# Batch 0's plain attention in two steps: q of two visits turned together, its last tokens' values behind a fifth w_in piece

## Chip, core and metric

The kernel runs on one core of one Trainium2 chip. The metric is the device time of that core, in microseconds (us), as the median of three runs. A core has TensorE (matmuls), VectorE, ScalarE and GpSimd (elementwise work) and a queue of DMA transfers that SyncE issues. In the profile they are called PE (its weight loads PEld), DVE, ACT, POOL and SP. Each engine works through its own list of instructions in order, and waits for the others by semaphores.

## What is computed

Attention over 8 batches, 8 heads, 576 tokens and 64 columns per head, and then a feed-forward layer over the 4608 tokens:

```python
scores = scale * np.matmul(q, k.transpose(0, 1, 3, 2))
mask_plain = (rel >= 0) & (rel < window)                     # window 32, heads 0 to 3
mask_dil = (rel >= 0) & (rel < window * dilation) & (rel % dilation == 0)   # dilation 4, heads 4 to 7
...
attn = np.exp(scores)
attn = attn / (np.sum(attn, axis=-1, keepdims=True) + 1e-09)
attn_out = np.matmul(attn, v)
...
h = x @ w_in                      # x: 4608 x 512, w_in: 512 x 2048
out = np.maximum(0.01 * h, h) @ w_out   # w_out: 2048 x 512
```

rel is the distance from a query back to a key, so each query sees 32 keys: the last 32 tokens in the plain heads, every fourth of the last 128 in the dilated ones. The inputs and the output are float32; the kernel multiplies in float16.

## The kernel before

**Stages and tiles.** Two batches make one block of 1152 tokens in `xt`, and a block is cut into three chunks of 384 tokens: chunk 0 holds the first 384 tokens of batch 0, chunk 1 those of batch 1, chunk 2 the last 192 of both. For each chunk, `up` (L778) makes 16 groups of up matmuls, one for each j: each group adds four matmuls of 128x384, one for each of four blocks of 128 rows of w_in (L792), into one of two banks `hps`, and ScalarE's leaky ReLU writes `gt` (L803). `down` (L827) makes three row blocks of 128 tokens, each of 16 matmuls of 128x512 in four parts of four (L841), into one of two banks `fps`; VectorE copies the sum to `osb` (L851), which goes to memory.

Attention of one batch is four visits of two heads, first the dilated pairs (2 and 3), then the plain ones (0 and 1). A visit has three units, u = 0, 1, 2. A unit makes a score bank of 384 columns on TensorE (L685, L669), its exponential on ScalarE (L691), a masking on VectorE (L705) or, for some units, a bias added on TensorE beforehand (L666), the value matmuls (L729, L739, L749) with row sums from a matrix of ones (L717), Ln and Exp on ScalarE for one over the sum (L761, L763), and the product on VectorE, which writes `xt` (L767).

**Batches 0 and 1 are early.** Their load is split: part 0 holds the units u = 0 and 1, which are the first 384 tokens, part 1 the unit u = 2. In part 0 of these two batches the value matmuls are half-width units: two sets of 64 columns side by side (L729 with `64x96` outputs, then L717). The q and k of a visit are cast to float16 in `nat`, turned by TensorE with an identity matrix into a bank (`tp` for q, `tpk` for k of batch 0, L557), and moved from there by VectorE or ScalarE into `slots` (L509, helper `move` at L503), where scores read them. For a plain visit q moves in four copies: two of 64x480 and two of 64x4x8, one of each for each head. The last 64 tokens (512 to 575) of all eight heads come separately: `load_rest` (L389) loads them into `rest`, TensorE turns all at once, and small copies put them into the slots (L583 on). The plain values of one batch are 24 tiles of 128 overlapping rows by 64 columns, six for each head: `load_group` (L306) loads them in two transfers of 12 tiles, one for each visit, as rows of 256 B, and GpSimd casts 12 tiles to `vp` (L379).

**Weights.** w_in comes in eight pieces of 512 KB, w_out in eight. Pieces 0 to 3 of w_in hold the columns of j = 0 to 7, pieces 4 to 7 those of j = 8 to 15, each piece one of the four row blocks. So a group j needs four pieces. Each piece is cast in two halves (L437).

**What sets the order.** All work is entered as tasks in a planner (L61 to L134), which gives each task an estimated duration, a priority and its dependencies, runs the engines' lists through an event loop, and so fixes one order on each engine; the instructions are then emitted in that order. The priority of the attention of a visit is `first + step * n`, with the pairs for batch 0 part 0, batch 0 part 1, batch 1 part 0 and batch 1 part 1 from `RANKS` (L21). The priority of loads of batches 0 and 1 and of all weights is the place in the string `FIRST` (L20, read at L873): b and v are q with k, and v, of one group of batch 0 (dilated first), c and y those of batch 1, i is a w_in piece, o a w_out piece, 0 and 1 the last tokens of batch 0 and batch 1. The masks that VectorE needs come with priority `CON` (L18) behind w_in's seventh piece. Where the planner sees a hole on TensorE before the down matmuls begin, matmuls on a constant tile fill it (L934); nothing reads their result.

**Names that the steps below touch.** `lv` and `v_late` (the loads of v, and what is left for later), `c_v` (the casts of v), `q_to` and `k_to` (the copies out of the turned banks), `turn` (L523) with its part 0 at L614, `unit` (L638). Only one bank, `sps`, holds scores after part 0 of batch 0, and two, `ops`, hold the values.

Of the kernel before, what the change touches and what calls it, by code (L numbers as in the profile page):

```python
# [16 lines left out]
WHEN = (-5.0, 15.0, 50.0, 77.0, 112.0, 138.0, 172.0, 200.0)  # L17
CON = -1484.5  # L18
AFTER = -1495.0
FIRST = "bvbviiii0iicooiicoyoooooy1"  # L20
RANKS = ((10.0, 1.0), (10.0, 3.0), (20.0, 2.0), (40.0, 0.5))  # L21


def _constants():
# [113 lines left out]
def kernel(  # L138
# [44 lines left out]
    def dram(t, off, *dims):  # L183
        return bass.AP(tensor=t.tensor, offset=t.offset + off, ap=[list(d) for d in dims])
# [48 lines left out]
                return n * (ta + (tb - ta) * (size - a) / (b - a)) / 16e3  # L233
        return n * size / 25.6 / 16e3

    def load(queue, dst, src, n, size, deps, prio):
        eng = ENG[queue]
        return plan.dma(queue, 0.7 if size == 128 else 0.48, took(n, size), deps,
                        lambda e: eng.dma_start(dst, src), prio,  # L239
                        LATE if prio > -1500 + len(FIRST) else 0.8 if prio >= AFTER else 0.0)  # L240

# [64 lines left out]
    def load_group(b, g, prio, prio_v):  # L306


        dil = g == 1
        early = b < EARLY  # L310
        first = b == 0
        base = (b * H + 4 * g) * HS
        stage, loads = [], []
        for o, src in ((0, q), (1, k)):
            sn, s_old = ring("STG", NST, s_users := [])
            st = stg[sn]
            if first:
                lo = [load("SP", at(st, 0, 128, j * 512, [256, 2], [1, 256]),
                           dram(src, base + 2 * j * HS, [4 * D, 128], [HS, 2], [1, 256]),
                           256, 1024, s_old, prio + 0.3 * j + 0.1 * o) for j in range(2)]  # L320
            elif early:
                lo = [load("SP", at(st, 0, 128, 0, [256, 4], [1, 256]),
                           dram(src, base, [4 * D, 128], [HS, 4], [1, 256]),
                           512, 1024, s_old, prio)]
            else:
                lo = [load("SP", at(st, 32 * a, 32 * a + 32, 0, [32, 36], [1, 32]),
                           dram(src, base + (a // 2) * 2 * HS + (a % 2) * 32,
                                [D, 32], [32 * D, 36], [1, 32]),
                           1152, 128, s_old, prio) for a in range(4)]
            stage.append((st, s_users))  # L330
            loads.append(lo)

        vn, v_old = ring("VST", NVS, v_users := [])
        vs = vst[vn]
        if dil and early:
            lv = [load("SP", at(vs, 0, 128, 0, [256, 4], [1, 256]),
                       dram(v, base, [4 * D, 128], [HS, 4], [1, 256]), 512, 1024, v_old, prio_v)]
            v_late[b] = vs, v_old, v_users
        elif dil:
            lv = [load("SP", at(vs, 0, 128, i * 256, [512, 4], [1, 256]),  # L340
                       dram(v, base + i * 64 * D, [4 * D, 128], [HS, 4], [1, 256]),
                       512, 1024, v_old, prio_v) for i in range(2)]
        elif early:
            lv = []
            for j in range(2):
                n = 12 - (first and j == 0)
                lj = [load("SP", at(vs, 0, 128, (12 * j + 12 - n) * D, [D, n], [1, D]),
                           dram(v, base + (1152 * j + 96 * (12 - n) - 32) * D, [D, 128], [96 * D, n],
                                [1, D]), 128 * n, 256, v_old, prio_v + 0.3 * j)]
                if n < 12:  # L350
                    lj += [load("SP", at(vs, PAD, 128, 0, [1, D]), dram(v, 0, [D, 96], [1, D]),
                                96, 256, v_old, prio_v), t_vz]
                lv.append(lj)
        else:
            lv = [load("SP", at(vs, 0, 128, 0, [D, 24], [1, D]),
                       dram(v, base - 32 * D, [D, 128], [96 * D, 24], [1, D]),
                       3072, 256, v_old, prio_v)]

        for j in range(2):
            nn, n_old = ring("NAT", NNAT, n_users := [])  # L360
            na, c_qk = nat[nn], []
            for o in range(2):
                st, s_users = stage[o]
                if early:
                    dst = at(na, 0, 128, o * 512, [D, 2], [128, 4], [1, D])
                    src = at(st, 0, 128, j * 512, [256, 2], [D, 4], [1, D])
                    n = 512
                else:
                    dst, src, n = na[:, o * S:o * S + S], st[:, j * S:j * S + S], S
                c_qk.append(cast(dst, src, n, (loads[o][j:j + 1] if first else loads[o]) + n_old, prio,  # L370
                                 (("ACT",) if o else ("DVE",)) if first and dil and j == 0 else
                                 CENG if early else ("POOL",)))
                s_users.append(c_qk[-1])
            dn, d_old = ring("VD" if dil else "VP", NV, d_users := [])
            vt = (vd if dil else vp)[dn]
            n_v = 384 if not dil else 256 if early else 512
            h_a, h_s = (2 * j * n_v, n_v) if early else (j * n_v, 2 * n_v)
            n, w = n_v // D, 128 * (8 if dil else 6)
            c_v = [cast(at(vt, 0, 128, 0, [w, 2], [128, n], [1, D]),  # L379
                        at(vs, 0, 128, h_a, [h_s, 2], [D, n], [1, D]), 2 * n_v,  # L380
                        (lv[j] if early and not dil else lv) + d_old, prio_v)]
            v_users += c_v
            seen_ones[b, 2 * g + j] = [t_ones["d" if dil else "p", dn]]
            kept[b, 2 * g + j] = vt, d_users
            visits[b, 2 * g + j, 0] = (na, c_qk, n_users, vt,
                                       c_v + ([t_one] if (b, 0) in TILED else
                                              [t_ones["d" if dil else "p", dn]]), d_users)

    def load_rest(b, prio):  # L389
# [5 lines left out]
        for o, src in ((0, q), (1, k)):  # L395
# [3 lines left out]
        c = cast(at(rest, 0, 128, 0, [128, 8], [D, 2], [1, D]),  # L399
                 at(st, 0, 128, 0, [D, 8], [0, 2], [1, D]), 1024, lo + r_old, prio)  # L400
        s_users.append(c)
        vs, v_old, v_users = v_late[b]
        spread = bass.AP(tensor=vs.tensor, offset=vs.offset + 1024,
                         ap=[[4 * vs.ap[0][0], 16], [256, 4], [1, 256]])
        lv = load("SP", spread,
                  dram(v, (b * H + 4) * HS + 512 * D, [4 * D, 16], [HS, 4], [1, 256]),
                  64, 1024, v_old + [t_vr], prio)
        for vi in (2, 3, 0, 1):
            vt, d_users = kept[b, vi]
            c_v = []  # L410
            if vi >= 2:
                c_v = [cast(at(vt, 0, 64, 0, [1024, 2], [128, 4], [1, D]),
                            at(vs, 0, 64, 1024 + (vi - 2) * 512, [256, 2], [D, 4], [1, D]), 512,
                            [lv] + d_users, prio + 30)]
                v_users += c_v
            visits[b, vi, 1] = rest, [c], r_users, vt, c_v + seen_ones[b, vi], d_users
# [3 lines left out]
    def load_w(n, prio):  # L420
# [10 lines left out]
        else:  # L431
            x = 1024 * (n - 8)
            src = dram(moe_w_out, 128 * x, [2 * DM, 128], [1, 1024])
            dst = w_out
        t = load("SP", st, src, 128, 4096, old, prio)
        for i in range(2):
            c = cast(dst[:, x + 512 * i:x + 512 * i + 512], st[:, 512 * i:512 * i + 512], 512, [t],  # L437
                     prio, ("POOL",) if 4 <= n < 8 else CENG)
# [71 lines left out]
        cost = {"DVE": 0.1 + n * 0.00065, "ACT": 0.08 + n * 0.00095}  # L510
        return add(tuple((e, cost[e]) for e in eng), None, 0.2, deps, fn, prio)

    slot_of, turned_rest, pair_moves = {}, {}, {}
    held = {t.name: [] for t in banks["S0"] + banks["O0"]}

    def arranged(dil, u0, u1):
# [6 lines left out]
    def turn(b, hp, part, prio):  # L523
# [50 lines left out]
        def k_to(bank, i, p0, p1, lo, hi, deps, eng=("DVE",)):  # L574
            n = hi - lo
            if dil:
                o, od, id_ = lo, [[144, 4], [1, n]], [[128, 4], [1, n]]
            else:
                o, od, id_ = PAD + 4 * lo, [[4, n], [1, 4]], [[1, n], [128, 4]]
            return [move(at(kb, p0, p1, o, *od), at(bank, p0, p1, i, *id_), 4 * n,  # L580
                         deps + old + zk, prio, eng)]

        if part == 1:  # L583
            if hp == 2:
# [26 lines left out]
            q_users += new  # L611
            ev += new
        else:
            _, q_old = ring("TP", 1, q_users := [])  # L614
            tq = add("PE", 0.23, 0.25, c_qk[:1] + [t_id] + q_old, turn_in(tpb, na, 0), prio, 0.2)
            n_users.append(tq)
            for lo, hi in ((0, 128),) if dil else ((0, 120), (120, 128)):
                q_users += q_to((lo, lo), lo, hi, [tq])
            if b == 0:
                _, k_old = ring("TPK", 1, k_users := [])  # L620
                kb_in, c_in, k_eng = tpk, 0, ("DVE", "ACT")
            else:
                k_old, k_users, kb_in, c_in, k_eng = q_old, [], tpb[:, 512:1024], 512, ("DVE",)
            tk = add("PE", 0.23, 0.25, [c_qk[1], t_id] + k_old, turn_in(kb_in, na, 512), prio, 0.2)
            n_users.append(tk)
            k_users += k_to(tpk if b == 0 else tpb, c_in, 0, 128, 0, 128,
# [3 lines left out]
            else:  # L630
                for t in q_users:
                    t.deps.append(tk)
                q_users += k_users
            ev += q_users + k_users
        slot_of[b, hp] = tn, users, ev
        return ev, users, qb, kb

# [347 lines left out]
```

The softmax here doesn't subtract the row's maximum and nothing guards it: scores larger than these inputs give would overflow.

## Time and profile before

The time is 317.56 us, the median of 317.21, 317.56 and 317.59. The profiled run has a span of 314.2 us, with TensorE's full clock granted throughout.

| engine | busy us | share of the span |
|---|---|---|
| TensorE, matmul | 303.7 | 97% |
| TensorE, weight load | 179.6 | 57% |
| ScalarE | 219.7 | 70% |
| VectorE | 174.2 | 55% |
| GpSimd | 120.4 | 38% |

| lines | what | count | busy us |
|---|---|---|---|
| L792 | up matmuls | 824 | 149.9 |
| L841 | down matmuls | 592 | 145.7 |
| L803 | leaky ReLU | 206 | 94.0 |
| L767 | product into xt | 138 | 52.4 |
| L509 | copies into the slots | 47 | 14.4 |

Transfers move 51.14 MB in all. Over the first 60 us they move 18.68 MB, at 311 GB/s on average. A row of a timeline has the start in us from the beginning of the span, the busy time, the engine, the line, the operation, what is written and read, the shape and how many instructions were merged; in brackets, the idle time of the engine just before and what ended it. TensorE's busy time includes the filler of L934 and of L863, so it is no measure of useful work in the first stage.

### The profile page before, as it was taken

How to read it: one execution, taken by the hardware profiler on the slowest of the kernel's cores; microseconds unless marked ns; L12 is line 12 of the kernel's file. 1: busy time of each engine (PE TensorE's matmuls, PEld its weight loads, DVE VectorE, ACT ScalarE, POOL GpSimd, SP SyncE). 2: the span in 40 equal slices, each digit the busy share in tenths (PEclk: the TensorE clock that was granted, in tenths of full speed). 3: DMA queues.
4: the chain of work that ended last, by engine and by line, in shares of the span. 5: the costliest groups of instructions: out<-in, count | busy, mean ns of one | idle time of the engine just before them, and what ended most of it. 6: DMA issues, size and time to landing. Idle time of an engine off the chain costs nothing.

```text
span 314.2 us, 6332 instructions
## 1 busy us (share of the span) xinstructions
PE 303.7 (97%) x2257; PEld 179.6 (57%) x2257; DVE 174.2 (55%) x396; ACT 219.7 (70%) x501; POOL 120.4 (38%) x174
## 2 busy tenths in 40 slices
PE   7968999999999999999999999999999999999995
PEld 3625555667777656655555555555555555555544
DVE  5856894557896687857858667654433420000011
ACT  3925674889998999987888888787887743334310
POOL 4466655464584463935819447450000000000000
PEclk9999999999999999999999999999999999999999
DMA  7999999999999399999989978711111111211113
GB/s 247 326 331 407 401 318 190 259 193 207 239 217 189 119 222 180 229 174 206 192 185 197 179 208 147 169 35 33 35 33 35 33 35 46 53 37 35 33 33 100
DMA packets 158175, 51.14 MB, mean 163 GB/s; under 512 B 139200, under 2 KB 151616, under 8 KB 158144
## 3 DMA queue, kind: packets, MB, share of 16 engines
q1 hardware_dynamic: 157696, 50.46, 67.3%
q8 instruction: 17, 0.28, 0.4%
q10 hardware_dynamic: 448, 0.29, 0.3%
q14 instruction: 14, 0.11, 0.1%
HBM read 41.30 MB, written 9.44 MB: 161 GB/s over the span
## 4 chain that ended last, share of the span: by engine, by line
PE 83%; DMA 7%; ACT 4%; SPq 3%; DVE 1%; issue 1%; POOL 0%; DVEq 0%
PE fps L841 38%; PE hps L792 36%; PE sps L685 3%; PE ops L749 3%; DMA wst<-in_moe_w_in_dram 3%; DMA con<-consts 3%; SPq L239 3%; ACT gt L803 1%; DMA stg<-in_k_dram 1%; ACT rc L761 1%; ACT rc L763 1%; PE ops L739 1%; PE sps L669 1%; DVE ee L705 1%; ACT ee L691 1%
## 5 line engine op out<-in xcount | busy, mean ns | idle before, releaser
L792 PE MATMUL hps<-xt,w_in 128*128 128x384 f16 (+1 forms) x824 | 149.9, 313 | 2.7 <-DVE w_in L249 1.3
L841 PE MATMUL fps<-w_out,gt 128*128 128x512 f16 (+1 forms) x592 | 145.7, 373 | 0.0
L803 ACT ACTIVATE gt<-hps 128x384 f16<-128x384 f32 (+1 forms) x206 | 94.0, 463 | 50.1 <-PE hps L792 46.1
L792 PEld LDWEIGHTS <-w_in 128*128 128x128 f16 x832 | 75.9, 98 | 46.0 <-DVE w_in L249 2.2
L841 PEld LDWEIGHTS <-gt 128*128 128x128 f16 x592 | 55.8, 98 | 45.1
L767 DVE TENSOR_TENSOR xt<-ops,rc 64x192 f16<-64x192 f32 (+2 forms) x138 | 52.4, 399 | 37.5 <-ACT rc L763 36.4
L544 POOL COPY slots<-turned 64x576 f16<-64x576 f16 x48 | 34.8, 724 | 59.6 <-DVE turned L539 47.0
L851 DVE COPY osb<-fps 128x512 f32<-128x512 f32 (+1 forms) x37 | 24.8, 671 | 55.7 <-PE fps L841 55.3
L705 DVE TENSOR_TENSOR ee<-ee,con 128x384 f16<-128x384 f16 x78 | 37.7, 487 | 30.9 <-ACT ee L691 29.7
L761 ACT ACTIVATE rc<-ops 64x384 f32<-64x384 f32 (+1 forms) x94 | 43.3, 464 | 13.7 <-PE ops L739 4.5
L691 ACT ACTIVATE ee<-sps 128x384 f16<-128x384 f32 x92 | 44.7, 486 | 9.8 <-PE sps L685 7.6
L763 ACT ACTIVATE rc<-rc 64x384 f32<-64x384 f32 (+1 forms) x96 | 46.7, 492 | 1.4
L249 POOL CAST nat<-stg 128x576 f16<-128x576 f32 (+1 forms) x52 | 34.9, 695 | 5.6 <-ACT ee L691 1.7
L685 PE MATMUL sps<-slots 128*128 128x192 f16 x152 | 25.0, 246 | 0.3 <-DVE slots L509 0.2
L685 PEld LDWEIGHTS <-slots 128*128 128x128 f16 x160 | 15.8, 102 | 11.7 <-issue 0.6
L249 POOL CAST vd<-vst 128x1024 f16<-128x1024 f32 (+2 forms) x20 | 17.5, 899 | 5.3 <-DMA vst<-in_v_dram 5.2
L550 DVE STREAM_TRANSPOSE slots<-nat 128x576 f16<-128x576 f16 x24 | 18.0, 762 | 1.3 <-POOL nat L249 1.1
L539 DVE STREAM_TRANSPOSE turned<-nat 128x576 f16<-128x576 f16 x24 | 18.1, 763 | 0.1
L509 DVE COPY slots<-tp 64x128 f16<-64x128 f16 (+5 forms) x47 | 14.4, 320 | 5.3 <-PE tp L557 4.6
L749 PEld LDWEIGHTS <-vp 128*128 128x128 f16 x160 | 11.1, 98 | 5.6
L249 POOL CAST vp<-vst 128x768 f16<-128x768 f32 x16 | 13.1, 832 | 2.9 <-DMA vst<-in_v_dram 2.2
L749 PE MATMUL ops<-ee,vp 128*128 128x96 f16 x160 | 13.3, 206 | 0.0
(64 smaller groups left out, 131.2 us busy)
## 6 DMA issues: line engine op xcount, KB each, us to landing
vst<-in_v_dram SPq DMA_DIRECT2D x14, 512.0 KB, 5.0
stg<-in_q_dram SPq DMA_DIRECT2D x48, 144.0 KB, 3.8
stg<-in_k_dram SPq DMA_DIRECT2D x48, 144.0 KB, 2.9
vst<-in_v_dram SPq DMA_DIRECT2D x6, 768.0 KB, 5.9
out_dram<-osb SPq DMA_DIRECT2D x16, 192.0 KB, 2.3
gt<-in_moe_w_in_dram SPq DMA_DIRECT2D x5, 512.0 KB, 7.0
out_dram<-osb SPq DMA_DIRECT2D x24, 96.0 KB, 2.1
out_dram<-osb SPq DMA_DIRECT2D x14, 128.0 KB, 2.6
```

The source lines that it names most:

```text
L249: ENG[e].tensor_copy(out=dst, in_=src)
L544: lambda e, p0=p0, hh=hh: nc.gpsimd.tensor_copy(out=at(qb, p0, p0 + 64, hh * S + o, *od), in_=at(xb, p0, p0 + 64, i, *id_)), prio)
L685: nc.tensor.matmul(st[:, 192 * i:192 * i + 192], ka, qa, start=not by_pe, stop=i == 1 or not by_pe)
L691: lambda e: nc.scalar.activation(out=et, in_=st[:, 0:384], func=AF.Exp, scale=SCALE), prio + 0.1)
L705: ENG[e].tensor_tensor(out=io, in0=io, in1=mk, op=ALU.mult)
L749: nc.tensor.matmul(ot[:, c:c + 96], va, et[:, c:c + 96], start=True, stop=True)
L761: lambda e: nc.scalar.activation(out=r_out, in_=r_in, func=AF.Ln), prio + 0.2)
L763: lambda e: nc.scalar.activation(out=r_out, in_=r_out, func=AF.Exp, scale=-1.0),
L767: nc.vector.tensor_tensor(out=dst, in0=at(ot, p0, p1, c, *i_), in1=at(rt, p0, p1, c, *i_), op=ALU.mult)
L792: nc.tensor.matmul(ht[:, 0:n], at(w_in, 0, 128, i * DFF + j // 2 * 256 + j % 2, [2, 128]), at(xt[m % 2], 0, 128, i * 1152 + x0 + x, [1, n] ...
L803: lambda e: nc.scalar.activation(out=gt[c % NG][:, j * n_c + x:j * n_c + x + n], in_=ht[:, 0:n], func=AF.Prelu, alpha=0.01),
L841: nc.tensor.matmul(ft[:, 0:n_o], g[:, j * n_c + tt * 128:j * n_c + tt * 128 + 128], w_out[:, j * DM + c0:j * DM + c0 + n_o], start=(j == 0 ...
```

## The change

Five edits, all around the first block.

- q of the two plain visits of batch 0 is turned into one bank: both sets of four transposes go into `tp`, 512 columns each, under one hold of that bank.
- Of each, the first 384 tokens are copied first (four copies of 64x384); tokens 384 to 511 of both visits follow in four further copies, of two visits each, which only the u = 2 units wait for. The k of the second plain visit is copied by VectorE alone and its priority is raised by 2.
- The plain values of batches 0 and 1 come in two parts: tiles 0 to 3 of each head in part 0, four transfers of four tiles, with casts of eight tiles; tiles 4 and 5 in `load_rest`, behind the last tokens, with a cast of their own.
- `FIRST` moves one w_in piece, the fifth, ahead of the last tokens of batch 0.
- `RANKS` has new steps for batch 0 part 1, batch 1 part 0 and batch 1 part 1. The planner's estimate for the transfer time of w_in's first four pieces is multiplied by 1.35, which only changes its order.

The aim is to have the first 384 tokens of batch 0 ready sooner, and the first w_in pieces with them: bytes and copies that only the last tokens need are taken out of the way of the first ones.

```diff
-FIRST = "bvbviiii0iicooiicoyoooooy1"
-RANKS = ((10.0, 1.0), (10.0, 3.0), (20.0, 2.0), (40.0, 0.5))
+FIRST = "bvbviiiii0icooiicoyoooooy1"
+RANKS = ((10.0, 1.0), (10.0, 2.0), (20.0, 1.0), (40.0, 2.0))
...
-            for j in range(2):
-                n = 12 - (first and j == 0)
-                lj = [load("SP", at(vs, 0, 128, (12 * j + 12 - n) * D, [D, n], [1, D]),
...
+            for h in range(4):
+                t0 = int(first and h == 0)
+                lv.append([load("SP", at(vs, 0, 128, (6 * h + t0) * D, [D, 4 - t0], [1, D]),
+                                dram(v, base + h * HS + (96 * t0 - 32) * D, [D, 128],
+                                     [96 * D, 4 - t0], [1, D]),
+                                128 * (4 - t0), 256, v_old, prio_v + 0.1 * h)])
...
+        ps, p_old, p_users = v_late[b, 0]
+        lp = [load("SP", at(ps, 0, 128, t * D, [6 * D, 4], [1, D]),
+                   dram(v, b * H * HS + (96 * t - 32) * D, [D, 128], [HS, 4], [1, D]),
+                   512, 256, p_old, prio) for t in (4, 5)]
...
+            if vi < 2:
+                c_v = [cast(at(vt, 0, 128, 4 * 128, [6 * 128, 2], [128, 2], [1, D]),
+                            at(ps, 0, 128, (12 * vi + 4) * D, [6 * D, 2], [D, 2], [1, D]), 256,
+                            lp + d_users, prio + 30)]
...
-        t = load("SP", st, src, 128, 4096, old, prio)
+        t = load("SP", st, src, 128, 4096, old, prio, 1.35 if n < 4 else 1.0)
...
+            if b == 0 and not dil:
+                if hp == 0:
+                    _, q_old = ring("TP", 1, q_users := [])
+                    both = []
+                    for x in range(2):
+                        n_x, c_x, u_x = visits[b, x, 0][:3]
+                        both.append(add("PE", 0.23, 0.25, c_x[:1] + [t_id] + q_old,
+                                        turn_in(tpb[:, 512 * x:512 * x + 512], n_x, 0), prio, 0.2))
+                        u_x.append(both[-1])
+                    two_q.append((both, q_users))
+                tq, q_users = two_q[0]
+                x = 512 * hp
+                made = q_to((x, x), 0, 96, tq)
+                q_users += made
...
+            if b == 0 and hp == 1:
+                later = []
+                for hh in range(2):
+                    p0 = 64 * hh
+                    for i, n, c in ((96, 24, 384), (120, 8, 480)):
+                        later.append(move(
+                            at(qbd[tn - 1], p0, p0 + 64, hh * S + c, [2 * S, 2], [24, 4], [1, n]),
+                            at(tpb, p0, p0 + 64, i, [512, 2], [128, 4], [1, n]), 8 * n,
+                            tq + zq + t_zero[tn - 1][0], prio + 30))
```

## Prediction

> **What bounds the kernel now.** I read four views in this order: busy time by stretch, to see which engine limits which stage; TensorE's timeline, to see where it waits or runs filler; the timelines of GpSimd and VectorE, to see what those waits end on; and the spacing of the small matmuls, because the change moves them. Columns of the first view: stretch, then busy us (count) of TensorE, weight load, VectorE, ScalarE, GpSimd, then clock, DMA share, GB/s.
>
> ```profile
> 17.12:25.00 7.88, 5.24 (x34) 2.71 (x33) 3.40 (x13) 2.18 (x7) 6.04 (x9) 1.00 1.02 352
> 25.00:35.00 10.00, 9.13 (x85) 5.36 (x82) 8.26 (x23) 4.37 (x10) 6.79 (x12) 1.00 1.06 407
> 35.00:50.00 15.00, 14.63 (x128) 8.18 (x126) 11.70 (x32) 11.06 (x29) 8.66 (x14) 1.00 0.97 314
> 50.00:100.00 50.00, 50.00 (x464) 34.19 (x459) 35.12 (x81) 42.59 (x113) 28.36 (x39) 1.00 1.07 218
> 100.00:200.00 100.00, 99.88 (x750) 59.46 (x746) 72.12 (x139) 87.73 (x192) 57.27 (x78) 1.00 0.93 188
> ```
>
> Two regimes: to about 34 us the DMA queue is full (share above 1.0) and TensorE has holes; from 36 us on TensorE never waits. The end is therefore the moment at which TensorE saturates plus a fixed list of matmuls. Work done sooner before 34 us only counts if useful matmuls replace filler there.
>
> ```profile
> 22.44 0.50 PE L792 MATMUL hps<-xt,w_in 128*128 128x384 f16 x2 [0.93 <-POOL w_in L249]
> 24.65 0.61 PE L557 MATMUL tp<-con,rest 128*128 128x128 f16 x8
> 26.72 0.70 PE L934 MATMUL fps<-warm 128*128 128x512 f16 x3
> 29.82 0.92 PE L934 MATMUL fps<-warm 128*128 128x512 f16 x4
> 31.46 1.03 PE L841 MATMUL fps<-w_out,gt 128*128 128x512 f16 x4
> 33.82 1.46 PE L792 MATMUL hps<-xt,w_in 128*128 128x384 f16 x8
> 35.66 0.40 PE L557 MATMUL tp<-con,nat 128*128 128x128 f16 x4 [0.37 <-DVE nat L249]
> ```
>
> L934 is filler. The up matmuls of the first half of w_in wait for its fourth piece (22.44); those of the second half start at 33.82 and need the eighth piece.
>
> ```profile
> 33.16 1.36 POOL L249 CAST w_in<-xt 128x512 f16<-128x512 f32 x2 [0.28 <-DMA xt<-in_moe_w_in_dram]
> 25.30 1.87 DVE L509 COPY slots<-tp 64x128 f16<-64x128 f16 x7 [2.53 <-PE tp L557]
> 27.20 0.76 DVE L249 CAST nat<-stg 128x512 f16<-128x512 f32 x2
> 28.30 0.43 DVE L249 CAST nat<-stg 128x512 f16<-128x512 f32 x1
> 30.92 0.42 DVE L249 CAST w_out<-wst 128x512 f16<-128x512 f32 x1
> 31.92 2.12 DVE L705 TENSOR_TENSOR ee<-ee,con 128x384 f16<-128x384 f16 x4 [0.58 <-DMA con<-consts]
> ```
>
> The eighth piece lands at 33.1 and its first cast ends at 33.84, just when the queue reaches it: two limits meet there. The other is VectorE's row: turned last tokens (25.30), batch 1's casts, w_out's cast (ends 31.34), down matmuls (31.46), 2.4 us of TensorE work, 33.82. Neither has slack.
>
> ```profile
> 42.69 0.28 PE L729 MATMUL ops<-ee,vd 128*64 128x96 f16 x4
> 42.80 0.25 PE L717 MATMUL ops<-ee,ones 128*64 128x192 f16 x2
> 42.98 0.40 PE L557 MATMUL tp<-con,nat 128*128 128x128 f16 x4
> 52.43 0.25 PE L729 MATMUL ops<-ee,vp 128*64 128x96 f16 x4
> 52.51 0.25 PE L717 MATMUL ops<-ee,ones 128*64 128x192 f16 x2
> 52.69 1.04 PE L841 MATMUL fps<-w_out,gt 128*128 128x512 f16 x4
> ```
>
> One half-width value unit alone: the four down matmuls before it start at 41.73 and take 0.87, so the unit and its two borders fill 42.60 to 42.98, 0.38 us. Two units side by side: eight down matmuls from 50.41 take 1.73, so the pair fills 52.14 to 52.69, 0.55 us. Splitting a pair costs 2 x 0.38 - 0.55 = 0.21 us.
>
> **What the Trainium skill says.** TensorEngine Tiling (Array Packing), Key Properties: changing the tiling mode drains TensorE. The trace agrees: the 0.21 us above is paid at the borders of the half-width units. DMA: Bandwidth & Descriptors, Specifications: transfers under 512 B don't reach line rate. The trace agrees: 284 to 290 GB/s while the 256-byte rows of v move (10.4 to 12.4 us), 409 on average from 26 to 42 us. Perfetto Trace Analysis, Sequencer Loop: an instruction waits for its semaphores in its engine's queue, so what stands behind it waits too. The trace agrees at 35.66, where up matmuls stand 0.37 us behind a transpose.
>
> **The change part by part.**
>
> Values in two parts: of 24 tiles of v, 8 go behind the w_in pieces: 8 x 128 = 1024 rows of 256 B, 0.26 MB. At 285 GB/s the first four w_in pieces land 0.92 us sooner. GpSimd casts 512 columns where it cast 768 (0.61 for 0.83 us, and 2 casts more later, at about 0.35 each beside DMA waits: nothing).
>
> q of two visits into one bank, 384 tokens copied first: in before each visit's q takes four VectorE copies, 1.20 us (the second at 13.55). Now four copies of 64x384 (about 0.34 each) serve both, and four small ones for tokens 384 to 511 come later. The second visit's scores move from 14.41 to about 13.4, its last xt from 17.88 to about 16.9. But the ups then wait for w_in, so this gives the same 0.9 us, not a second one. From 22.44 the ups move to 21.5.
>
> Fifth w_in piece ahead of the last tokens: the pieces are the same, and the constants (mask), w_out's first pieces and the eighth w_in piece stand behind the same bytes as before. 33.16 stays. In the changed program's order TensorE does the same set of matmuls before the second-half ups; only filler grows (8 more of 512, 4 fewer of 256). So the 0.9 us ends in filler. Hidden by: the transfers up to 33.1.
>
> What it costs there: the turning of the last tokens now stands behind all four ups of j 4 to 7 instead of between them. They start at 23.36 - 0.92 = 22.44 and take 4 x 0.65, with 0 to 0.25 us of waiting for a bank: 25.04 to 25.3 against 24.65. VectorE's seven copies (1.87) start 0.4 to 0.6 later; one cast (0.38) has left VectorE for GpSimd. The k cast at 28.30 comes 0 to 0.2 later, and everything behind it up to the ups at 33.82. One copy now also stands ahead of the masks and delays them to about 32.4. I take 0.3 us at the j = 10 up (range 0 to 0.4).
>
> RANKS: batch 1's first part gets a denser rank. In the order of TensorE the tiled units of batch 1 are now eight single ones instead of four single and two pairs: 2 x 0.21 = 0.43 us (0.4 to 0.46; surely on the path, since TensorE is saturated).
>
> The same re-ranking moves the last units of batch 1 right in front of the ups of chunk 1, which need their xt. Before: the last unit's values at 52.43, xt done at 54.09, the up at 54.88: 0.7 us spare. Changed order on TensorE: last unit, four scores, four down matmuls, four scores, eight values, two scores, up. On VectorE: a mask, then the copy of those very down matmuls (osb), then the last xt. From the start s of the down group: it ends at s + 0.87, a copy starts 0.2 after that (46.60, 47.47, 47.67 in before), takes 0.68, xt 0.35, the up 0.06 later: s + 2.16. TensorE's own work between: 0.87 + 0.17 + 0.20 + 0.17 = 1.41. A wait of 0.75 us that wasn't there; with the mask (0.36) and the one score bank (0.49 of Exp before it is free) ahead, 0.8. Low end 0.3, if the scheduler's slack elsewhere has delayed TensorE there; high end 1.2. Queued behind it: every later up.
>
> Sum: 0 (start) + 0.3 + 0.43 + 0.8 = 1.5 us; 317.56 + 1.5 = 319.06.
>
> **The rivals.**
> Faster: the transfers from 13 to 22 us run at 215 to 390 GB/s instead of 409. If the new order removes such a dip, the eighth piece and the constants land sooner too and the 0.92 us is kept while the waits stay away: 317.56 - 0.92 = 316.6. For: the dips are in the queue that limits. Against: the same transfers follow each other.
> No change: only the split pairs cost, the other two terms hide in each other: 317.56 + 0.43 = 318.0. For: 33.84 stays. Against: the chain through the osb copy is fixed by order, not by how early TensorE comes.
> Slower by more: score, Exp, mask, value, Ln, Exp, xt of batch 1 now stand closer together on two ops banks, with waits at more of the eight units: 1.0 us more, 320.1. For: before it had 0.7 us spare at one place only. Against: between units stand 0.86 us down groups.
>
> **How the numbers follow.** Forecast 0.60, faster 0.12, no change 0.16, slower by more 0.12. The forecast and the last lie beyond 318.2, slower by over 0.2%: 0.72. No change 0.16, faster 0.12. The range leaves out the faster case and the far end of the last: low ends of the terms, 0 + 0.4 + 0.3 less 0.5 for the dips give 317.7, taken to 317.4; high ends 0.4 + 0.46 + 1.2 and 0.9 for more waits give 320.5.
>
> **What would show it.** Right: the fourth w_in piece's up at 21.5, more L934 filler between 25 and 31, the second-half ups at 33.8 to 34.1; single half-width units with 0.38 us each; a wait for VectorE's xt at the first ups of chunk 1, near 57. Wrong: the eighth piece's cast well before 32.5 or after 34; no wait near 57; new waits after 60.

## The result, and the profile after

The changed kernel takes 320.8 us in the median (319.86, 320.63, 320.97, 322.76), 3.2 us above the kernel before; over all executions the ratio is 1.0112, 95% interval 1.0064 to 1.016. The forecast was 319.0 and the range ended at 320.5: the direction was right, the size was not. In a second comparison, with 6 runs of the changed kernel and 43 of the kernel before on another chip, the ratio is 1.0069 (1.0043 to 1.0095), that is 2.2 us. The kernel before took between 316.4 and 317.0 us on the chips of the experiments, so each experiment is given as its ratio to the kernel before on its own chip. Two traces below, of e2 and e15, are from a slow state with a granted clock of 0.848, and no times are read from them.

Busy time by stretch after the change, same columns as in the prediction:

```profile
17.12:25.00 7.88, 5.49 (x31) 2.71 (x30) 3.74 (x14) 2.17 (x7) 3.99 (x8) 1.00 0.99 320
25.00:35.00 10.00, 8.70 (x68) 4.87 (x67) 6.34 (x19) 3.72 (x8) 7.87 (x14) 1.00 1.03 357
...
50.00:100.00 50.00, 48.89 (x435) 32.09 (x434) 35.27 (x80) 41.18 (x105) 25.82 (x37) 1.00 1.01 208
```

Two things changed. The transfers move 320 and 357 GB/s where they moved 352 and 407, so what has to come from memory comes later. And TensorE, which had no hole between 50 and 100 us, now has 1.11 us of them there.

TensorE's timeline after the change:

```profile
35.54 1.46 PE L837 MATMUL hps<-xt,w_in 128*128 128x384 f16 x8
...
37.64 0.40 PE L568 MATMUL tp<-con,nat 128*128 128x128 f16 x4 [0.64 <-DVE nat L249]
...
41.72 0.48 PE L837 MATMUL hps<-xt,w_in 128*128 128x384 f16 x2 [0.20 <-ACT gt L848]
...
58.52 0.36 PE L784 MATMUL ops<-ee,vd 128*128 128x48 f16 x8 [0.35 <-DVE ee L750]
...
59.51 1.30 PE L837 MATMUL hps<-xt,w_in 128*128 128x384 f16 x7 [0.27 <-DVE xt L812]
...
79.33 0.33 PE L794 MATMUL ops<-ee,vd 128*128 128x96 f16 x4 [0.44 <-DVE ee L750]
```

The second-half ups start at 35.54 instead of 33.82. Behind them come four waits that are new or longer: 37.64 (0.64, was 0.37), 41.72, the pair at 58.52 and 59.51, and 79.33.

What stands before the ups, on GpSimd, TensorE and VectorE:

```profile
34.82 1.33 POOL L249 CAST w_in<-xt 128x512 f16<-128x512 f32 x2 [0.30 <-DMA xt<-in_moe_w_in_dram]
```

```profile
26.63 0.61 PE L568 MATMUL tp<-con,rest 128*128 128x128 f16 x8
```

```profile
27.28 1.85 DVE L520 COPY slots<-tp 64x128 f16<-64x128 f16 x7 [4.45 <-PE tp L568]
...
32.64 0.42 DVE L249 CAST w_out<-wst 128x512 f16<-128x512 f32 x1
...
33.94 2.41 DVE L750 TENSOR_TENSOR ee<-ee,con 128x384 f16<-128x384 f16 x4
```

The eighth w_in piece is cast at 34.82 instead of 33.16. But the ups don't start by it: the first half of its cast ends at 35.47, and the matmul that needs it, the fourth of its group, begins at 36.02 (33.83 and 34.31 before). They start by VectorE's row. The turn of the last tokens is 1.98 us late (26.63 for 24.65), so VectorE's copies are (27.28 for 25.30), its cast of w_out is 1.72 us late (32.64 for 30.92), and the ups follow that cast by 2.90 us in both traces, as they do in nine traces of the experiments (2.89 or 2.90).

**A count that splits the span.** From the first of the second-half ups to the last matmul both traces hold the same 2,025 matmul records (800 up, 584 down, 201 score, 416 value, 24 turns), in another order. That stretch, from the start of the one to the start of the other, called the list below, takes 276.34 us before and 278.52 after: 2.18 us. The start of it moved by 1.72. Together that is the 3.9 us between the two spans (314.2 and 318.1); the trace of the kernel before is of an execution of 315.94 us, 1.6 below the median of 317.57 beside the result, so the 3.9 are more than the 3.2 of the medians. A second trace of the changed kernel (e5) has the same order: its list takes 278.43 and starts at 34.58, again 2.90 us behind the cast of w_out (31.68). Within the list, each matmul's distance to the next, less what is usual for its kind, gives: borders of half-width units 0.43 more; the two places at chunk 1 together 0.91; 37.64 0.26 more; 41.72 0.36; 79.33 0.53; 90.04 0.21; less 0.45 for two waits of the kernel before (at 110.5 and 131.9) that are gone. Sum 2.25, close to the 2.18.

### The profile page after: what moved, and what is told of

It is laid out like the page before. It is cut to its first block, busy times and chain, and to the rows that moved or that the text cites. A ratio compares the mean times of both kernels' runs of the same rounds, so it can differ in the third digit from the quotient of the medians.

```text
span 318.1 us, 6353 instructions
## 1 busy us (share of the span) xinstructions
PE 306.4 (96%) x2261; PEld 180.1 (57%) x2261; DVE 174.1 (55%) x397; ACT 220.1 (69%) x501; POOL 118.9 (37%) x177
## 4 chain that ended last, share of the span: by engine, by line
PE 85%; DMA 5%; DVE 4%; ACT 3%; SPq 2%; issue 1%; DVEq 0%
PE fps L886 38%; PE hps L837 37%; PE sps L730 3%; PE ops L794 3%; DMA wst<-in_moe_w_in_dram 3%; DMA stg<-in_q_dram 2%; DVE slots L520 2%; SPq L239 2%; ACT gt L848 1%; PE tp L568 1%; PE ops L784 1%; DVE ee L750 1%; ACT rc L806 1%; PE sps L714 1%; ACT rc L808 1%
## 5 line engine op out<-in xcount | busy, mean ns | idle before, releaser
L520 DVE COPY slots<-tp 64x128 f16<-64x128 f16 (+7 forms) x47 | 14.2, 319 | 7.8 <-PE tp L568 7.2
L249 POOL CAST vp<-vst 128x768 f16<-128x768 f32 (+2 forms) x20 | 14.2, 724 | 2.2 <-DMA vst<-in_v_dram 1.1
```

The source lines that it names most:

```text
L249: ENG[e].tensor_copy(out=dst, in_=src)
```

## The experiments

The first theory was: the stream is late because of the many small transfers (1.7 us), and the list is longer because of `RANKS` (1.2 to 1.8 us). The table has what was measured; the last two columns are from the profiled run of each kernel.

| kernel | ratio to before, 95% | list starts | list takes |
|---|---|---|---|
| before | 1 | 33.82 | 276.34 |
| e5, changed kernel again | 1.0069 (1.0043 to 1.0095) | 34.58 | 278.43 |
| e1, changed, old RANKS | 1.0077 (1.0055 to 1.0099) | 36.52 | 278.14 |
| e2, before, new RANKS | 1.0013 (0.9996 to 1.003) | | |
| e3, changed, values as before | 1.0077 (1.0054 to 1.01) | 36.81 | 277.87 |
| e4, before, values in more transfers | 1.0029 (1.0016 to 1.0042) | 35.13 | 276.23 |
| e6, changed, no factor | 1.0009 (0.9992 to 1.0026) | 35.60 | 276.17 |
| e7, before, factor 1.35 | 1.0056 (1.0039 to 1.0072) | 34.93 | 278.32 |
| e8, before, q and fifth piece | 1.0026 (1.0015 to 1.0037) | 35.59 | 276.19 |
| e9, before, fifth piece | 1.0018 (0.9999 to 1.0037) | 36.74 | 276.21 |
| e10, before, q in one bank | 0.9987 (0.9964 to 1.001) | 35.23 | 276.25 |
| e11, before, single units | 1.0048 (1.0027 to 1.0069) | 34.21 | 277.85 |
| e12, before, values in two parts | 1.0048 (1.0029 to 1.0068) | 35.73 | 277.20 |
| e13, e6 with late values later | 1.0025 (1.0011 to 1.0038) | 34.64 | 276.58 |
| e14, changed, chunk 1 clear | 1.0034 (1.0017 to 1.0051) | 34.33 | 277.33 |
| e15, before, factor 0.9 | 1.0045 (1.0019 to 1.0071) | | |

The column of starts mixes two kinds of trace. In those of e1, e3, e4, e6, e9, e10 and e12 TensorE's granted clock is 0.50 for 3.41 us, somewhere between 19.7 and 34.6 us (last section); in those of before, after, e5, e7, e8, e11, e13 and e14 it isn't, and only starts of one kind can be compared. The ratios mix such executions too. Of executions with a mean clock of 0.997 or more alone, the kernel before has a median of 316.3 to 316.4 us on each of the four chips; above it are e5 by 2.4 us, e6 by 0.3, e7 by 2.2, e9 by 0.8, e13 by 0.9 and e15 by 1.8.

**Is it RANKS?** e1 undoes it in the changed kernel, e2 does it alone.

```diff
-RANKS = ((10.0, 1.0), (10.0, 2.0), (20.0, 1.0), (40.0, 2.0))
+RANKS = ((10.0, 1.0), (10.0, 3.0), (20.0, 2.0), (40.0, 0.5))
```

> The changed kernel with RANKS of the kernel before. Theory (two causes that add: a late stream, 1.7 us, and the denser ranks, 1.2 to 1.8 us): the ranks' share goes, the second-half ups still start at 35.5, the wait for xt at chunk 1's first ups (0.27 us) and the split pairs go: 319.0 to 319.6 us. Rival (all of it is the late stream, and what is lost after 36 us only follows from it): 320.8 as in the changed kernel.

> The kernel before with RANKS of the changed kernel alone. Theory (the denser ranks cost on their own): second-half ups at 33.8 as before, then 1.2 to 1.8 us more: 318.8 to 319.4 us. Rival (ranks cost only after a late stream): 317.6.

The theory misses in both; e2's rival, no cost, holds. With the old ranks the changed kernel is no faster (2.4 us above the kernel before), its eight half-width units stay single, and the wait for xt is still there, at 59.89. With the new ranks alone the kernel before keeps four single units and two pairs and loses at most 1 us, perhaps nothing. By itself RANKS is not the cause.

**Is it the transfers of the values?** e3 loads them as before; e4 only cuts them up, with every engine's list unchanged.

```diff
-                n = 12 - (first and j == 0)
-                lj = [load("SP", at(vs, 0, 128, (12 * j + 12 - n) * D, [D, n], [1, D]),
...
+                lj = [load("SP", at(vs, 0, 128, (6 * h + x) * D, [D, y - x], [1, D]),
...
+                      for x, y in ((t0, 4), (4, 6))]
```

> The changed kernel with the plain values loaded as before, in two transfers of 12 tiles ahead of w_in. Theory (the many small transfers make the stream late, because only eight transfers can be open and each new one waits for the eighth before it): eighth w_in piece cast at about 33.2 and second-half ups at 33.8 although 0.26 MB more stand ahead of w_in: 319.1 us. Rival (the fifth piece ahead of the last tokens or the new q copies make it late): 35.5 and 320.8.

> The kernel before with each batch's plain values cut into eight transfers instead of two, the same bytes at the same place and the same order on every engine. Theory (number of transfers counts): w_in's first pieces and the eighth one 0.5 to 1.7 us later, 318.1 to 319.3 us. Rival (only bytes count): 33.2 for the eighth piece and 317.6.

e3 misses (2.4 us above, no better than the changed kernel): its eighth piece is cast at 33.87, near the 33.2 that the theory named, and its ups still start at 36.81, behind the fall of the clock. e4 holds at its low end, 0.9 us, and shows by what: SyncE's queue issues nine transfers of v, where it issued three, before it comes to w_in. In e4, and then in the kernel before:

```profile
6.28 5.76 SPq L239 DMA_DIRECT2D vst<-in_v_dram  x9
12.09 0.94 SPq L239 DMA_DIRECT2D gt<-in_moe_w_in_dram  x2
```

```profile
9.99 2.23 SPq L239 DMA_DIRECT2D gt<-in_moe_w_in_dram  x2
```

Six transfers more, and w_in's first piece is issued 2.1 us later. So the count of transfers costs, but it can't be most of the 2.2 to 3.2 us.

**Is it the planner's estimate?** The list of TensorE with one edit at a time has eight single units with the factor 1.35 alone (e7), and four (and two pairs) with new RANKS, the fifth piece or the new q alone (e2, e9, e10). The planner's list for the values in two parts with q has eight too, with the old RANKS or the new; with the new RANKS and the fifth piece together the pairs are back, as long as the factor is not there (of these only the last was run, as e6). So: e6 takes the factor out of the changed kernel, e7 puts it alone into the kernel before; e5 is the changed kernel beside them.

```diff
-        t = load("SP", st, src, 128, 4096, old, prio, 1.35 if n < 4 else 1.0)
+        t = load("SP", st, src, 128, 4096, old, prio)
```

> The changed kernel itself, beside the kernel before on the chip of this group, so that the others can be compared with it. Both theories: 3.2 to 3.6 us above the kernel before, second-half ups at about 35.5.

> The changed kernel without the planner's factor 1.35. The transfers keep their order to 30 us, TensorE's list has four single half-width units and two pairs again, and chunk 1's ups stand clear of the last unit. Theory (two separate losses: late stream 1.7 us, a list of TensorE rearranged by the planner's estimate 1.8 us): second-half ups still at 35.5, the rest as in the kernel before: 1.5 to 1.9 us above it. Rival (RANKS did it, which is kept here): 3.2 us above it.

> The kernel before with the factor 1.35 alone. The transfers keep their order to 30 us; TensorE's list has eight single half-width units and the last one right ahead of chunk 1. Theory: second-half ups at 33.8 as before, then 1.4 to 1.8 us more behind them. Rival (the waits at chunk 1 only come with a late stream): 0.4 us more, from the split pairs alone.

This settles the larger part. Without the factor the changed kernel is 0.3 us above the kernel before (1.0009, interval 0.9992 to 1.0026), better than the theory expected; the factor alone makes the kernel before 1.8 us slower, at the upper end of its theory. Its list takes 1.98 us more, although nothing but the planner's estimate differs; its ups start at 34.93, not at the expected 33.8. e5 misses what was expected of it, 3.2 to 3.6 us: it has 2.2. Chunk 1 in e7:

```profile
57.78 0.33 PE L669 MATMUL sps<-slots 128*128 128x96 f16 x4 [0.58 <-ACT ee L691]
...
58.53 1.30 PE L792 MATMUL hps<-xt,w_in 128*128 128x384 f16 x7 [0.26 <-DVE xt L767]
```

Scores wait for the one score bank, where in the changed kernel value matmuls wait for a mask; then the ups of chunk 1 wait for the last xt, as there. In e6 the last units are a pair, and a down group, a turn and a down group stand between them and the ups, which do not wait:

```profile
53.26 0.28 PE L774 MATMUL ops<-ee,vp 128*64 128x96 f16 x4
53.37 0.25 PE L762 MATMUL ops<-ee,ones 128*64 128x192 f16 x2
53.45 0.25 PE L774 MATMUL ops<-ee,vp 128*64 128x96 f16 x4
53.54 0.25 PE L762 MATMUL ops<-ee,ones 128*64 128x192 f16 x2
53.72 1.04 PE L886 MATMUL fps<-w_out,gt 128*128 128x512 f16 x4
54.59 0.61 PE L568 MATMUL tp<-con,rest 128*128 128x128 f16 x8
55.04 1.03 PE L886 MATMUL fps<-w_out,gt 128*128 128x512 f16 x4
55.90 1.46 PE L837 MATMUL hps<-xt,w_in 128*128 128x384 f16 x8
```

**Does the size of the factor matter?** e15 has 0.9 instead of 1.35.

```diff
-        t = load("SP", st, src, 128, 4096, old, prio)
+        t = load("SP", st, src, 128, 4096, old, prio, 0.9 if n < 4 else 1.0)
```

> The kernel before with the factor 0.9 instead of 1.35 on w_in's first four pieces: the planner now thinks them early, not late. Transfers keep their order; TensorE's list is nearly that of e7, eight single units, the last one right ahead of chunk 1. Theory (any shift of the estimate undoes the list that the kernel before has): 1.8 to 2.2 us slower, as e7. Rival (only an estimate that is too long costs): within 0.3 us of the kernel before.

1.4 us slower (0.6 to 2.2). The theory named 1.8 to 2.2 and the interval holds that; the rival's 0.3 is outside. A shorter estimate undoes the list as a longer one does: it has eight single units too. So it isn't only that 1.35 is too pessimistic; both other estimates that were run lose the list of before.

**Which part of the list?** e11 splits the pairs in the kernel before; e14 was meant to change the changed kernel only from chunk 1 on.

```diff
-RANKS = ((10.0, 1.0), (10.0, 3.0), (20.0, 2.0), (40.0, 0.5))
+RANKS = ((10.0, 1.0), (10.0, 3.0), (20.0, 1.0), (40.0, 0.5))
```

> The kernel before with one number of RANKS changed, the step of batch 1's first part 1.0 instead of 2.0: all eight half-width units are single, and chunk 1's ups keep their distance of a turn and a down group from the last unit. Transfers as before. Theory (two split pairs cost 0.21 us each): 0.4 us more. Rival (the split costs nothing and the factor's loss is all in the waits at chunk 1): within 0.15 us of the kernel before.

```diff
-RANKS = ((10.0, 1.0), (10.0, 2.0), (20.0, 1.0), (40.0, 2.0))
+RANKS = ((10.0, 1.0), (10.0, 3.0), (20.0, 1.0), (40.0, 2.0))
```

> The changed kernel with one number of RANKS, the step of batch 0's second part, 3.0 instead of 2.0. TensorE's list stays the same up to chunk 1, with eight single half-width units; from there a down group and four scores stand between the last unit and chunk 1's first up. Theory (the chain through the osb copy at chunk 1 costs 0.9 us): 1.3 to 1.6 us above the kernel before, where the changed kernel has 2.4. Rival (the loss is in the split pairs and what stands before 57 us): 2.2 to 2.4 us above it.

e11 fails as a clean test: 1.5 us, not 0.4. Its borders do cost 0.43 more, but its list also gets a wait of 0.42 at chunk 1 (56.59), since one down group fewer stands there, and several of 0.2 to 0.3 elsewhere. e14 comes out 1.1 us above the kernel before, where the changed kernel has 2.2: its list takes 277.33, with the eight single units and without a wait at chunk 1 or at 79. The theory's 1.3 to 1.6 lie within its interval (0.5 to 1.6), the rival's 2.2 to 2.4 outside. The order of e14 differs from the third microsecond of the list on, not only from chunk 1; but over the list's first 18 us both kernels lose the same, borders left out (1.24 and 1.27 us over what is usual for the matmuls there). So the order around chunk 1 and behind it is worth about 1.1 us, the split pairs 0.43.

**And the start?** e8, e9, e10 and e12 take the other edits one or two at a time; e13 moves the late transfers of v behind the sixth w_in piece.

```diff
-FIRST = "bvbviiii0iicooiicoyoooooy1"
+FIRST = "bvbviiiii0icooiicoyoooooy1"
```

> The kernel before with q of two visits in one bank and the fifth w_in piece ahead of the last tokens; values, RANKS and the factor as before. The number and order of the other transfers stay and TensorE's list behind the second-half ups is that of the kernel before. Theory (only transfers and list cost): within 0.4 us of the kernel before. Rival (the piece's place makes the stream late): second-half ups near 35 and 1.2 us more.

> The kernel before with the fifth w_in piece ahead of the last tokens, nothing else; TensorE's list behind the second-half ups stays. Theory (e8's loss is this piece: the turn of the last tokens and all behind it comes later): 0.6 to 0.9 us more, second-half ups about 1 us later than in the kernel before. Rival (the loss of e8 is the new q copies): within 0.3 us of the kernel before.

> The kernel before with q of two visits in one bank, nothing else. Theory (ups wait for w_in, not for xt): within 0.3 us of the kernel before. Rival: 0.8 us more, as in e8.

> The kernel before with plain values in two parts, alone, and steps of RANKS (2, 1.5) chosen so that six units are single and chunk 1's ups stand clear of the last unit. Theory (eight tiles fewer ahead of w_in bring it sooner): first w_in piece's cast about 1 us sooner, second-half ups 0.5 to 0.9 us sooner, less 0.2 us for a split pair: 0.3 to 0.7 us faster than the kernel before. Rival (more small transfers cost as much as the missing bytes bring): 0.2 us slower or the same.

```diff
-                   512, 256, p_old, prio) for t in (4, 5)]
+                   512, 256, p_old, prio if b else -1488.5) for t in (4, 5)]
```

> The changed kernel without the factor (as e6), and of batch 0 the two late transfers of v behind the sixth w_in piece instead of ahead of it; TensorE, VectorE and ScalarE keep e6's lists. Theory (a transfer waits for the eighth before it, so small ones ahead of the sixth piece hold it back): the sixth piece is issued at about 17 instead of 20 us, second-half ups up to 0.5 us sooner than in e6: within 0.2 us of the kernel before, or 0.3 us faster. Rival (the bytes ahead of the eighth piece are the same, so nothing moves): 0.3 us slower than the kernel before, as e6.

q in one bank costs nothing, as expected. The fifth piece alone costs 0.6 us (0 to 1.2), as e9's theory had it, and with q 0.8, where e8's theory allowed 0.4. In e9 the turn of the last tokens starts at 26.23 instead of 24.65, and VectorE's copies behind it at 28.60 instead of 25.30, since a cast ahead of them waits for its transfer until 27.62. The values in two parts, alone, miss: 1.5 us slower, of which 0.9 is in its list, and its first ups run into a wait of another kind. VectorE and TensorE of e12:

```profile
19.77 0.43 DVE L249 CAST w_in<-wst 128x512 f16<-128x512 f32 x1 [2.66 <-DMA wst<-in_moe_w_in_dram]
20.11 0.35 DVE L810 TENSOR_TENSOR xt<-ops,rc 128x192 f16<-128x192 f32 x1
```

```profile
20.51 0.97 PE L835 MATMUL hps<-xt,w_in 128*128 128x384 f16 x5 [2.56 <-DVE xt L810]
```

The last xt stands on VectorE behind a cast that waits 2.66 us for its transfer, and TensorE behind both. The Trainium skill, Perfetto Trace Analysis, Sequencer Loop, says that an instruction waits for its semaphores after it has been put into its engine's queue; the trace agrees, and shows the cost for what is queued behind it, here with VectorE in the middle.

e13 refutes the idea about the small transfers: the sixth piece is issued at 15.54 instead of 19.95, and nothing comes of it; the eighth is cast at 34.49, and the kernel is 0.8 us above the one before. What stands ahead of the eighth piece is the same, so the rival was right that nothing is gained; why e13 is rather slower than e6 is in part seen: the order of the two lists is the same, but e13's takes 0.41 us more, and 0.33 of that is the wait for VectorE's k cast (0.69 us at 36.87, where e6 has 0.36 at 37.42). The rest stays open. So does why the losses of the parts at the start (0.6 to 0.9 us each in e4, e8 and e9) don't add up in e6, which has nearly all of them and loses 0.3.

No version beat both kernels: e10's 0.9987 can't be told from 1.

## Why the prediction was right in direction and wrong in size and cause

The sum was 1.5 us. The first pair of traces has 1.72 us at the start of the list, where the sum has nothing, and 2.18 in the list. The second trace of the changed kernel has 0.76 and 2.09.

- **Values in two parts, w_in 0.92 us sooner; turn of the last tokens, 0.3 us.** This is the step that failed, in the sum "0 (start) + 0.3". It had the fourth piece 0.92 us sooner, the ups of j = 4 to 7 from 22.44 and the turn behind them at 25.04 to 25.3. Only the first piece came sooner: its cast at 15.29 for 15.98, but the third and fourth at 20.43 and 22.43 for 19.79 and 21.52, while the transfers moved 320 GB/s instead of 352. So these ups start at 23.80, the turn at 26.63, and the delay goes through VectorE's row to the second-half ups: 1.72 us there. In the second trace of the changed kernel the fourth piece is cast at 21.34, the turn is at 25.54 and the ups start 0.76 us late: the start costs too much there as well. The part of the term that was put at the j = 10 up is right: its wait grew from 0.37 to 0.64. How much of this the edit costs on the average stays open: two traces are no mean, and e6, with the changed transfers and the pairs of before, is only 0.3 us above the kernel before over 22 executions.
- **"33.16 stays", 0 us.** As a landing time this is wrong too (34.82, and 34.56 in the second trace). But it isn't what moved the ups: the prediction saw two limits meet and gave neither slack, while the eighth piece had 0.48 us before and 0.55 after. In the second trace the ups start at 34.58, before the first half of the cast ends (35.17). And e10 casts the piece at 33.22, with ups at 35.23.
- **RANKS, split pairs, 0.43 us.** The size was right to the hundredth (0.43 in borders, eight single units). It was read from the changed list itself, so it holds whichever edit made the list. The cause was wrong: e2 shows that RANKS alone splits no pair. The changed list was read as a whole and given to the edit that looked like it. The factor 1.35 was given no term at all; the description of the change says that it only changes the planner's order, and that order is what cost.
- **Chunk 1 behind the osb copy, 0.8 us.** Measured 0.91, at 58.52 and 59.51. Right in place, chain and size, and again put down to RANKS where e7 has the wait for xt from the factor alone.
- **"New waits after 60" as a sign of being wrong.** There is one, at 79.33 (0.53), and one before chunk 1 that was not listed, at 41.72 (0.36), where a group of ups waits for ScalarE to empty its bank; ScalarE has done two steps of one over the sum just before. With 90.04, and less the waits of the kernel before that went, they are the rest of the list's 2.18 us against the 1.5 of the sum. The sum had nothing for them, and that is the other term that failed: 0.65 us net.

Of the rivals, "slower by more" was nearest, 320.1, but not for its stated reason: it had waits at the units of batch 1 on the ops banks, and the waits found beyond the forecast are at 41.72 and 79.33, and before the list starts.

## What to carry to other kernels

Where a planner fixes the order, an estimated duration is an edit to every engine's list: build the kernel with each edit alone, and with the others, and compare the lists before a cost is given to any of them. A tuned list can be lost by a small edit: here two other estimates and one other rank cost 1.4 to 1.8 us, while three single edits left TensorE's order as it was (e4, e9, e10). Where two limits seem to meet, look for the distance that stays the same in other traces, here 2.90 us from VectorE's cast to the ups. And a time from a single profile has a spread of its own: two traces of the changed kernel start the list 0.96 us apart. Don't write 0 for a term that rests on one.

## What the hardware showed that was not expected

The wait at 79.33 comes from one VectorE instruction. GpSimd and VectorE of the changed kernel there:

```profile
77.11 0.72 POOL L555 COPY slots<-turned 64x576 f16<-64x576 f16 x1 [0.97 <-DVE turned L550]
77.77 1.29 POOL L249 CAST nat<-stg 128x576 f16<-128x576 f32 x2
```

```profile
77.67 1.60 DVE L750 TENSOR_TENSOR ee<-ee,con 128x384 f16<-128x384 f16 x1
```

The mask takes 1.60 us instead of 0.36; it begins while a GpSimd copy runs and ends just after the GpSimd casts (79.06). The second run of the changed kernel has it again, 1.59 us. The Trainium skill, SBUF — State Buffer, "SBUF: two separate sides", says that the port pair that the two share is an exclusive lock between a VectorE instruction with two SBUF inputs and a GpSimd instruction that reads SBUF. This trace agrees: of its 80 masks of this shape, the 39 that meet no GpSimd instruction take 0.34 to 0.36 us, and 28 of the other 41 take over 0.40. The kernel before has such masks too, up to 1.18 us; this one is the longest, and TensorE waits for it.

In e9 TensorE's clock fell, and the list starts at 36.74. Stretches of e9, the third number from the end being the granted clock:

```profile
28.00:30.00 2.00, 0.19 (x5) 0.19 (x6) 1.96 (x7) 0.00 (x0) 1.70 (x3) 1.00 1.01 409
30.00:32.00 2.00, 1.70 (x16) 1.10 (x14) 1.72 (x6) 0.98 (x2) 1.16 (x2) 0.60 1.03 399
32.00:34.00 2.00, 2.00 (x14) 1.27 (x12) 1.48 (x4) 0.53 (x2) 1.47 (x3) 0.55 1.09 392
```

After a stretch with 0.19 of 2 us busy the clock is 0.50 from 30.40 to 33.81, just where the matmuls ahead of the second-half ups stand. The Trainium skill, TensorE: Matmul & The Clock Gate, Part 1, says that a window of some 3.4 us of idleness halves the clock. The length agrees, 3.41 us, but less idleness was enough here: the longest holes before the seven falls are 1.71 (e3) to 2.56 us (e12), and TensorE was busy for 27 to 44% of the 3.41 us before each (41 and 47% in e15 and e2). A hole alone doesn't decide it: the changed kernel has one of 2.02 us (19.33 to 21.35) and no fall. In steps of 3.41 us counted back from the fall behind the last matmul, no stretch of the eight traces without an early fall is busy for less than 45% before 45 us. So in these traces the fall goes with a step that is busy for less than about half, not with a hole of a certain length, and where a hole lies in the steps matters. Of the 199 executions of the kernel before beside the experiments, 63 have a mean clock under 0.997, and their median is 1.1 to 1.8 us above that of the others on their chip. So the filler of L934 is part of the path: holes of about 2 us that it leaves can cost more than themselves.
